# Moving the second half of a weight conversion from the MLP of batch 0 into the attention

## The chip, the core and the metric

The program runs on one NeuronCore of a Trainium2 chip. The metric is the device time of one execution in microseconds (us). The core has five engines with a queue of instructions each: TensorE (PE; its weight loads are listed apart, as PEld), VectorE (DVE), ScalarE (ACT), GpSimd (POOL) and SyncE (SP, which here only starts DMA transfers). An engine takes its instructions in the order of its queue and waits on semaphores for what the others produce. TensorE writes to PSUM, which has eight banks; DVE and ACT read it from there.

## What is computed

The reference is a hash-bucketed attention followed by an FNet block, for 4 batches, 8 heads, 768 positions and 64 dimensions a head:

```
q_bits = (q @ proj) > 0;  k_bits = (k @ proj) > 0        # 6 bits each
mask   = bucket(q) == bucket(k)
attn   = softmax(where(mask, q k^T / 8, -1e9));  o = attn @ v
x  = o as (batch, 768, 512)
u  = x + real(fft over positions and channels of x)
un = (u - mean) / sqrt(var + 1e-6)
out = u + relu(un @ w_ch1) @ w_ch2                       # 512 -> 2048 -> 512
```

The two weight matrices reach the kernel as float64. The kernel reads them as pairs of 32-bit integers and makes float32 of them itself.

## The kernel before

**Two phases.** `attention` handles 16 pairs of heads (n = 0 to 15, four for each batch). Then come, for each of the four batches, `mix` (the Fourier transforms as matmuls, L1045) and `mlp7` (L1342). The MLP multiplies 2x2 blocks with seven products instead of eight (Strassen-Winograd). `inner` makes the hidden layer (L1400), `outer7` the output (L1279); each runs twice per batch, for the first and the second half of the hidden features: inner half 0, outer half 0, inner half 1, outer half 1.

**Order.** The attention is emitted under a manual schedule: every engine executes its instructions in the order in which the code emits them. A pair has six steps, c = 0 to 5. In a step TensorE computes the bucket masks and the scores of 128 keys against all queries (L846, L856), ACT turns them into exponentials in a ring of four buffers `pk` (L862), TensorE multiplies the exponentials of the step before by v (L872), and DVE adds those to a running sum (`tally`, L929). Between these lie, at set steps, the end of the pair before (`scale`: ACT copies at c = 0, TensorE sums at c = 1, reciprocals at c = 2, for batches 0 and 1 the division at c = 3) and the preparation of the next pair (`prepare`: DVE transposes q at c = 0 and k at c = 1, ACT squares q at c = 1 and k at c = 2, TensorE asks for the bits of q at c = 2 and of k at c = 3, DVE tells them one step later). PSUM is full: two score tiles of two banks, two output banks, and two banks (`ps_1`) for everything else. Outside the attention the framework's planner arranges the instructions of each engine by its own costs; `in_turn` ties a weight step behind the last MLP instructions recorded in `done_by`.

**Weights.** `w1` (512 x 2048) comes in 16 slices of 128 x 512, four for each group of 512 columns. `Arrival` keeps transfers of 512 KB ahead in a few raw buffers. `convert` turns one raw slice into float32 with `narrow` (L610): two DVE operations on the high words (L622, L626), three ACT operations (L630, L632, L633, the last with an accumulator read), and, one visit later, a DVE integer addition (L636). After four slices `centred` subtracts the column averages: four matmuls `ws` (L651), an ACT copy to `part`, one matmul `wm` (L659), and four DVE subtractions (L665) in two visits. A generator gives out one such step at a visit: two visits for a slice, four for the centring of a group.

The generator `other` in the attention is `weights1`, on the groups at columns 0 and 1024. It is visited once at the head of pair 1 (where its first transfers start) and at c = 0 and c = 5 of every later pair. The groups at 512 and 1536 are in `weights2`, between the two halves of w2: in batch 0, outer half 0 visits it twice at each of its eight yields. Its transfers go out on the POOL queue. The left factors of inner half 1 (`quarters(HF // 2)`, L1479) need them.

**Fold.** `fold(b)` (L956) makes even and odd parts of a batch's x for the Fourier transform, on DVE, in eight steps for batch 0. The attention visits `fold(0)` at c = 1 from pair 5 on; the folds of later batches run in the MLP of the batch before. `fold` and `part` share one buffer, tag `ef`.

Of the kernel before, what the change touches and what calls it, by code (L numbers as in the profile page):

```python
# [11 lines left out]
F32 = mybir.dt.float32  # L12
# [8 lines left out]
P = 128  # L21
B, H, S, D = 4, 8, 768, 64
NBITS = 6
DM = H * D
DFF = 4 * DM
NT = S // P
NPAIR = H // 2
# [3 lines left out]
NDC = DM // P  # L31
GTT = 2
GT = GTT * P
WC = 512
# [443 lines left out]
def _main(  # L478
# [13 lines left out]
    nc = tc.nc  # L492
# [11 lines left out]
    def wt(shape, dtype, tag, name, bufs=2):  # L504
        return work.tile(shape, dtype, tag=tag, name=name, bufs=bufs)
# [140 lines left out]
    def average(f):  # L646


        ps = pt([P, WC], f"ws{f}")
        for c in range(NDC):  # L650
            nc.tensor.matmul(  # L651
                ps[32 * c : 32 * c + 32, :], ones, w1[:, c, f : f + WC],
                start=True, stop=True,
            )
        part = wt([P, 2, S], F32, "ef", f"part{f}", 1)[:, 0, 0:WC]
        nc.scalar.copy(part, ps)
        yield
        ps = pt([P, WC], f"wm{f}")
        nc.tensor.matmul(ps, mean, part, start=True, stop=True)  # L659
        yield ps  # L660
# [9 lines left out]
    @contextmanager  # L670
    def in_turn():

        with ExitStack() as st:
            for ins in done_by.values():
                st.enter_context(tc.issue_after(ins.ins))
            yield
# [35 lines left out]
    def slices1(fs):  # L712
        return [
            (w1[:, c, f : f + WC], moe_w_ch1[c * P : (c + 1) * P, f : f + WC])
            for f in fs
            for c in range(NDC)
        ]

    def centred(f):

        avg = average(f)
        next(avg)
        yield
        ps = next(avg)
        yield
        for c in range(0, NDC, 2):
            centre(f, ps, (c, c + 1))
            yield

    def weights1():  # L730
        fs = (0, DFF // 2)
        slices = slices1(fs)
        zt = at_([P, 3, 2 * WC], F32, "zraw", "zraw1", 1)
        arrival = Arrival(slices, [zt[:, i] for i in range(3)], 0, nc.sync)
        for i in range(arrival.depth):
            arrival.fetch(i)
        yield
        for i in range(len(slices)):
            low = wt([P, WC], I32, "u", f"low{i}")
            yield from arrival.convert(i, low)  # L740
            yield
            if i % NDC == NDC - 1:
                yield from centred(fs[i // NDC])
# [248 lines left out]
    def attention(other):  # L992

        pending, ends = [], []
        load(1, "qk")
        for n in range(NPAIR * B):
            b, t = divmod(n, NPAIR)
            if t == 0:
                xs[b] = wt([P, NPAIR, S], F32, "x", f"x{b}", B)
            if n + 2 < NPAIR * B:  # L1000
                load(n + 2, "qk")
            if n + 1 < NPAIR * B:
                load(n + 1, "v")
            if n == 1:
                next(other)
            if n == NPAIR + 1:
                folds = fold(0)
            if n == 6:
                nc.sync.dma_start(ch, cn["ch"].ap())
                nc.sync.dma_start(sq, cn["sq"].ap())  # L1010
            ahead = prepare(n + 1) if n + 1 < NPAIR * B else iter(())
            oos = [ps_o.tile([P, 512], F32, tag="o", name=f"oo{n}_{g}") for g in range(2)]
            acc = at_([P, 2, 2, HALF], F32, "acc", f"acc{n}")
            first = None
            for c in range(NT):
                pk = scores(n, c)
                first = pk if c == 0 else first
                done = pending.pop(0) if pending else None
                if c == 1:
                    next(ends[0][0], None) if ends else None  # L1020
                if done:
                    m, d, dpk, doos, dfirst, dacc = done
                    values(m, d, dpk, doos)
                    tally(d, dpk, dfirst, dacc)
                    if d == NT - 1:
                        ends.append([scale(m, doos, dacc, None)])
                        next(ends[-1][0])
                if ends and c in (2, 3):
                    next(ends[0][0], None)
                    if c == 3:  # L1030
                        ends.pop(0)
                if c < NT - 1 if n else c:
                    next(ahead, None)
                if n > 1 and c in (0, NT - 1):
                    next(other, None)
                if n > NPAIR and c == 1:
                    next(folds, None)
                pending.append((n, c, pk, oos, first, acc))
        m, d, dpk, doos, dfirst, dacc = pending.pop(0)
        values(m, d, dpk, doos)  # L1040
        assert next(other, 0) == 0 and next(folds, 0) == 0
        for _ in scale(m, doos, dacc, dpk):
            pass
# [103 lines left out]
    HF = NFC // 2  # L1147
# [53 lines left out]
    def weights2():  # L1201

        slices = []
        for half in range(2):
            for r in range(HF // 2):
                for hi, first in ((0, B11), (1, B21)):
                    c = half * HF // 2 + r + hi * HF

                    step = 1 if hi else T1 - B11
                    dst = w2f[:, 0 : 7 * QB].rearrange("p (i r n) -> p i r n", i=7, n=HD)  # L1210
                    slices.append(
                        (dst[:, first : first + step + 1 : step, r],
                         moe_w_ch2[c * P : (c + 1) * P, :])
                    )
        fs = (WC, DFF // 2 + WC)
        n1 = len(fs) * NDC
        slices[HF:HF] = slices1(fs)
        arrival = Arrival(slices, [zt2[:, i] for i in range(2)], n1, nc.gpsimd)
        for half in range(2):
            if half == 0:  # L1220
                for i in range(arrival.depth):
                    arrival.fetch(i)
                yield
            else:
                for i in range(n1):
                    with in_turn():
                        for _ in arrival.convert(HF + i):
                            pass
                    yield
                    if i % NDC == NDC - 1:  # L1230
                        steps = centred(fs[i // NDC])
                        while True:
                            with in_turn():
                                if next(steps, 0) == 0:
                                    break
                            yield
            for i in range(HF):
                with in_turn():
                    for _ in arrival.convert(half * (HF + n1) + i):
                        pass  # L1240
                yield
                if i % 2:
                    b11, b21, b22, t4, t1, t2, t3 = (q[:, i // 2] for q in right7)
                    with in_turn():
                        nc.vector.tensor_tensor(t3, b22, t1, op=ALU.subtract)
                        nc.vector.tensor_tensor(t1, t1, b11, op=ALU.subtract)
                        nc.vector.tensor_tensor(t2, b22, t1, op=ALU.subtract)
                        nc.vector.tensor_tensor(t4, b21, t2, op=ALU.subtract)
            for i in range(7):
                nc.sync.dma_start(bd[half, i], right7[i])  # L1250
            if half == 0:
                yield
# [89 lines left out]
    def mlp7(b):  # L1342
# [134 lines left out]
        for half in range(2):  # L1477
            if b == 0 and half:
                quarters(HF // 2)  # L1479
            for i, _ in enumerate(inner(half)):  # L1480
                if b == 0 and half and i % 3 < 2:
                    next(arrival2, None)
                yield
            if b == 0 and half == 0:
                for T in range(3):
                    across(b, T, ut[T])
            if b == 0 and half == 0:
                ahead, per = islice(arrival2, 2 * (NDC + 4)), 2
            elif half == (b == 0) and b < B - 1:
                ahead, per = fold(b + 1), 1  # L1490
            else:
                ahead, per = iter(()), 0
            for _ in outer7(b, half, hall, ut, rs, ss):
                for _ in range(per):
                    next(ahead, None)
                yield
            for _ in ahead:
                pass
# [13 lines left out]
    for b in range(B):  # L1512
# [22 lines left out]
        if b == 0:  # L1535
            zt2 = wt([P, 3, 2 * WC], F32, "z", "zraw2", 1)
            arrival2 = weights2()
# [48 lines left out]
```

## Time and profile before

| | us |
|---|---|
| median of 3 runs (1059.22 to 1062.81) | 1059.47 |
| the profiled execution | 1059.36 |
| its span, first to last instruction | 1057.6 |
| TensorE busy | 1031.1 (97%) |
| VectorE busy | 677.3 (64%) |
| ScalarE busy | 500.4 (47%) |
| GpSimd busy | 69.4 (7%) |

In the rows that follow, a line of the timeline or of the chain gives start and duration in us, engine, source line, operation, output<-input and count, and in brackets the idle time before it with what ended it. A row of a table by stretches gives the stretch (us from the start of the span), its length, the busy time of PE, PEld, DVE, ACT and POOL with the number of instructions, the clock granted to TensorE (1.00 is full), the busy share of the DMA engines and the rate. A row of groups gives line, engine, operation, tiles, shapes and count, then busy us and mean ns of one, then idle us before them.

### The profile page before, as it was taken

How to read it: one execution, taken by the hardware profiler on the slowest of the kernel's cores; microseconds unless marked ns; L12 is line 12 of the kernel's file. 1: busy time of each engine (PE TensorE's matmuls, PEld its weight loads, DVE VectorE, ACT ScalarE, POOL GpSimd, SP SyncE). 2: the span in 40 equal slices, each digit the busy share in tenths (PEclk: the TensorE clock that was granted, in tenths of full speed). 3: DMA queues.
4: the chain of work that ended last, by engine and by line, in shares of the span. 5: the costliest groups of instructions: out<-in, count | busy, mean ns of one | idle time of the engine just before them, and what ended most of it. 6: DMA issues, size and time to landing. Idle time of an engine off the chain costs nothing.

```text
span 1057.6 us, 14425 instructions
## 1 busy us (share of the span) xinstructions
PE 1031.1 (97%) x5169; PEld 646.0 (61%) x5169; DVE 677.3 (64%) x1214; ACT 500.4 (47%) x1009; POOL 69.4 (7%) x147
## 2 busy tenths in 40 slices
PE   8999999999999999889999999999999999999997
PEld 4333333333333655555688587689678589678576
DVE  4777878887665398848988854446854354644353
ACT  5677766877666567526513512402521512430420
POOL 2000000000000001200020200020200012200000
PEclk9999999999999999989999999999999999999999
DMA  9534442434210137344642305323314315223301
GB/s 136 119 78 94 83 103 45 101 59 82 46 39 13 41 125 257 99 128 133 245 134 101 98 18 187 92 71 132 92 45 160 105 41 174 70 70 112 107 20 43
DMA packets 172464, 103.03 MB, mean 97 GB/s; under 512 B 126304, under 2 KB 159584, under 8 KB 172384
## 3 DMA queue, kind: packets, MB, share of 16 engines
q1 hardware_dynamic: 165216, 83.92, 29.5%
q0 software_dynamic: 5600, 17.70, 5.6%
q8 instruction: 43, 0.70, 0.3%
q10 hardware_dynamic: 1568, 0.39, 0.2%
q14 instruction: 37, 0.30, 0.1%
HBM read 81.01 MB, written 20.97 MB: 96 GB/s over the span
## 4 chain that ended last, share of the span: by engine, by line
PE 53%; DVE 3%; DMA 2%; ACT 1%; issue 1%; DVEq 0%
PE o L1279 26%; PE h_p L1400 21%; PE cs L1061 2%; PE B L1090 1%; PE A L1090 1%; DMA zraw<-in_moe_w_ch_dram 1%; PE un L1116 1%; PE ws L651 1%; DVE w L626 0%; DMA ad<-tq 0%; PE wm L659 0%; DVE w L1291 0%; DVE w L639 0%; DVE u L1291 0%; DVE w L622 0%
## 5 line engine op out<-in xcount | busy, mean ns | idle before, releaser
L1279 PE MATMUL o<-w,h 128*128 128x256 f32 x1152 | 256.1, 381 | 0.5 <-ACT tq L1298 0.3
L1279 PEld LDWEIGHTS o<-w,h 128*128 128x128 f32 x1152 | 220.2, 191 | 33.8 <-issue 1.5
L862 ACT ACTIVATE pk<-sc 128x768 f32<-128x768 f32 x192 | 153.6, 810 | 91.7 <-PE sc L856 91.7
L1400 PE MATMUL h_p<-x,w 128*128 128x384 f32 x448 | 160.5, 488 | 2.0 <-ACT h L1440 1.8
L856 PE MATMUL sc<-qt,kt 64*128 64x384 f32 x768 | 155.2, 483 | 0.0
L872 PE MATMUL oo<-pk,vn 128*64 128x385 f32 (+1 forms) x768 | 145.1, 498 | 0.0
L929 DVE TENSOR_TENSOR acc<-acc,pk 128x1536 f32<-128x1536 f32 x63 | 110.2, 1750 | 38.6 <-ACT pk L862 38.5
L1400 PEld LDWEIGHTS h_p<-x,w 128*128 128x128 f32 x448 | 84.0, 190 | 60.4 <-ACT h L1440 6.7
L1400 PE MATMUL h_p<-w 128*128 128x384 f32 x288 | 104.8, 487 | 0.0
L872 PEld LDWEIGHTS oo<-pk,vn 128*64 128x64 f32 x768 | 46.7, 136 | 87.8 <-issue 76.8
L856 PEld LDWEIGHTS sc<-qt,kt 64*128 64x128 f32 x768 | 68.6, 189 | 21.7 <-issue 21.5
L1400 PEld LDWEIGHTS h_p<-w 128*128 128x128 f32 x288 | 54.5, 190 | 37.4 <-PE un L1116 0.4
L1291 DVE SCALAR_TENSOR_TENSOR w<-o,rs,w 128x256 f32<-128x256 f32 x56 | 26.9, 481 | 65.6 <-PE o L1279 64.8
L846 PE MATMUL sc<-qkb 64*128 64x384 bf16 x384 | 63.9, 328 | 1.0 <-ACT pk L862 0.5
L846 PEld LDWEIGHTS <-qkb 64*128 64x128 bf16 x384 | 18.8, 93 | 73.0 <-issue 58.6
L1309 ACT COPY tq<-o 128x256 f32<-128x256 f32 x24 | 8.9, 371 | 103.3 <-PE o L1279 103.3
L1414 ACT ACTIVATE h<-h 128x384 f32<-128x384 f32 x72 | 37.7, 524 | 33.6 <-DVE h L1456 14.1
L929 DVE TENSOR_TENSOR acc<-pk,pk 128x1536 f32<-128x1536 f32 x16 | 28.1, 1759 | 39.8 <-ACT pk L862 39.8
L1298 ACT COPY tq<-o 128x256 f32<-128x256 f32 x24 | 8.8, 367 | 74.3 <-PE o L1279 74.3
L1451 DVE TENSOR_TENSOR h<-h 128x384 f32<-128x384 f32 x32 | 17.8, 557 | 40.4 <-ACT h L1450 40.4
L1279 PE MATMUL o<-w 128*128 128x256 f32 x176 | 41.6, 380 | 0.0
L1440 ACT COPY h<-h_p 128x384 f32<-128x384 f32 x32 | 15.2, 476 | 46.1 <-PE un L1116 24.0
(158 smaller groups left out, 1308.8 us busy)
## 6 DMA issues: line engine op xcount, KB each, us to landing
w<-ad SPq DMA_DIRECT2D x168, 128.0 KB, 2.0
w<-bd SPq DMA_DIRECT2D x42, 512.0 KB, 4.6
zraw<-in_moe_w_ch_dram POOLq DMA_DIRECT2D x24, 512.0 KB, 4.3
bd<-w SPq DMA_DIRECT2D x14, 512.0 KB, 3.5
vn<-in_v_dram SPq DMA_DIRECT2D x32, 192.0 KB, 3.0
qn<-in_q_dram SPq DMA_DIRECT2D x116, 48.0 KB, 2.3
kn<-in_k_dram SPq DMA_DIRECT2D x58, 96.0 KB, 3.0
zraw<-in_moe_w_ch_dram SPq DMA_DIRECT2D x8, 512.0 KB, 4.0
```

What stands on the lines that cost most here:

```text
L846: nc.tensor.matmul(ps[:, h, 0:HALF], qk[rows, 1, at : at + P], qk[rows, 0, g * HALF : (g + 1) * HALF], start=start, stop=not start,)
L856: nc.tensor.matmul(ps[:, h, 0:HALF], kt[rows, ks], qt[rows, qs], start=early, stop=not early,)
L862: nc.scalar.activation(pk[:, g, :, 0:HALF], ps[:, :, 0:HALF], AF.Exp, scale=SCALE)
L872: nc.tensor.matmul(oos[g][h * D : (h + 1) * D, 0:w], nat["v", n][:, (2 * c + h) * D : (2 * c + h + 1) * D], pk[:, g, h, 0:w], start=(c == ...
L929: nc.vector.tensor_tensor(acc, (first[:, :, :, 0:HALF] if c == 1 else acc), new, op=ALU.add)
L1061: nc.tensor.matmul(ps[:, pc + 2 * lo : pc + 2 * hi - 1 : 2], z[:, cp, pc, par, t * P : (t + 1) * P], ch[:, cp, pc, lo:hi], start=(cp == 0) ...
L1090: nc.tensor.matmul(ps[:, cols], F[:, par, k, t, j * P : (j + 1) * P], sq[:, t, k, cols], start=(t == 0), stop=(t == 1),)
L1279: nc.tensor.matmul(ps, a[:, r], right7[i][:, r], start=start and r == 0, stop=r == HF // 2 - 1, skip_group_check=not start,)
L1291: nc.vector.scalar_tensor_tensor(t[:, cols], src, r, t[:, cols], op0=ALU.mult, op1=ALU.add)
L1400: nc.tensor.matmul(ps, left[:, k], right[i][:, k], start=start and k == 0, stop=k == 1, skip_group_check=not start,)
L1414: done_by[ET.Activation] = nc.scalar.activation(h, h, AF.Relu)
L1451: done_by[ET.DVE] = nc.vector.tensor_tensor(c22, c21, c22, op=ALU.add)
```

## The change

`weights1` takes all 16 slices, and the attention visits it at c = 0, 1, 4 and 5 of a pair, from c = 4 of pair 1 on. `weights2` keeps only w2, and outer half 0 of batch 0 visits nothing. `part` moves from the buffer `ef` to tag `u`, which has two buffers and which it shares with `low`. `fold(0)` starts in pair 9 instead of 5, with one visit at c = 1 of each pair and a second one in pairs 13, 14 and 15 (at c = 5, 4 and 3).

```diff
@@ average
-        part = wt([P, 2, S], F32, "ef", f"part{f}", 1)[:, 0, 0:WC]
+        part = wt([P, WC], F32, "u", f"part{f}", 2)
@@ weights1
-        fs = (0, DFF // 2)
+        fs = range(0, DFF, WC)
@@ attention
-            if n == NPAIR + 1:
+            if n == 2 * NPAIR + 1:
                 folds = fold(0)
...
-                if n > 1 and c in (0, NT - 1):
+                if n and c in (0, 1, 4, 5) and n + c > 2:
                     next(other, None)
-                if n > NPAIR and c == 1:
+                if n > 2 * NPAIR and (c == 1 or n + c == 18):
                     next(folds, None)
@@ weights2
-        fs = (WC, DFF // 2 + WC)
-        n1 = len(fs) * NDC
-        slices[HF:HF] = slices1(fs)
-        arrival = Arrival(slices, [zt2[:, i] for i in range(2)], n1, nc.gpsimd)
+        arrival = Arrival(slices, [zt2[:, i] for i in range(2)], NDC * DFF // WC, nc.gpsimd)
         for half in range(2):
             if half == 0:
...
-            else:
-                for i in range(n1):
-                    with in_turn():
-                        for _ in arrival.convert(HF + i):
-                            pass
-                    yield
-                    if i % NDC == NDC - 1:
-                        steps = centred(fs[i // NDC])
-                        while True:
-                            with in_turn():
-                                if next(steps, 0) == 0:
-                                    break
-                            yield
             for i in range(HF):
                 with in_turn():
-                    for _ in arrival.convert(half * (HF + n1) + i):
+                    for _ in arrival.convert(half * HF + i):
                         pass
@@ mlp7
-            if b == 0 and half == 0:
-                ahead, per = islice(arrival2, 2 * (NDC + 4)), 2
-            elif half == (b == 0) and b < B - 1:
-                ahead, per = fold(b + 1), 1
-            else:
-                ahead, per = iter(()), 0
+            ahead = fold(b + 1) if half == (b == 0) and b < B - 1 else iter(())
             for _ in outer7(b, half, hall, ut, rs, ss):
-                for _ in range(per):
-                    next(ahead, None)
+                next(ahead, None)
                 yield
```

## The prediction, made before the changed kernel was built or run

> **What bounds the kernel now.** I read the page's head first, for the engine that fills the span.
>
> ```profile
> span 1057.6 us, 14425 instructions
> PE 1031.1 (97%) x5169; PEld 646.0 (61%) x5169; DVE 677.3 (64%) x1214; ACT 500.4 (47%) x1009; POOL 69.4 (7%) x147
> ```
>
> TensorE is busy 97% of the time, so a change pays only where TensorE waits or runs slowly, or where it saves matmuls. The next view is the table by stretches, cut where the stages of batch 0 begin and end: outer half 0 (417.31 to 476.44), two pieces of it, inner half 1 after it, and as the yardstick outer half 0 of batch 1, which has the same products and no weight work.
>
> ```profile
> 417.31:476.44 59.13, 50.60 (x191) 34.78 (x190) 39.98 (x83) 23.02 (x47) 10.93 (x20) 0.88 0.43 139
> 428.76:438.55 9.79, 5.49 (x12) 1.00 (x12) 6.91 (x15) 4.80 (x9) 4.45 (x9) 0.83 0.39 116
> 450.72:461.23 10.51, 6.74 (x11) 1.34 (x11) 3.83 (x7) 4.81 (x9) 1.06 (x2) 0.65 0.75 236
> 476.44:517.47 41.03, 38.08 (x114) 20.74 (x113) 35.39 (x87) 31.39 (x69) 3.17 (x6) 1.00 0.57 183
> 610.36:646.62 36.26, 36.26 (x170) 31.98 (x169) 17.73 (x35) 4.65 (x12) 0.00 (x0) 1.00 0.24 79
> ```
>
> The stage lasts 59.13 us in batch 0 and 36.26 us in batch 1, where TensorE never pauses. The difference of 22.87 us sits mostly in the two short pieces, which are the two centrings: TensorE is idle for 4.30 and 3.77 us in them and the granted clock falls to 0.83 and 0.65. The waits of TensorE in this stage say for what:
>
> ```profile
> PE ws L651 <- DVE w L636: 6.7, 2, 3.6
> PE wm L659 <- ACT part L656: 1.3, 2, 0.7
> PE o L1279 <- ACT tq L1298: 0.3, 1, 0.3
> ```
>
> The column sums `ws` stand in TensorE's queue and wait for the last slices of their group to be converted (6.7 us), `wm` waits for the copy (1.3 us), and the MLP's products stand behind both. Last, the attention, in stretches from one `sum` matmul to the next, that is one pair each: pairs with one slice (first and fourth row), with a `ws` (second), with a `wm` (third), and one late pair without weights (last).
>
> ```profile
> 99.86:121.19 21.33, 21.33 (x146) 8.29 (x145) 17.74 (x22) 16.18 (x30) 0.00 (x0) 1.00 0.40 82
> 121.19:143.52 22.33, 22.33 (x154) 8.46 (x153) 18.11 (x27) 16.37 (x30) 0.00 (x0) 1.00 0.43 88
> 143.52:165.91 22.39, 22.39 (x149) 8.60 (x147) 18.35 (x23) 14.41 (x26) 0.00 (x0) 1.00 0.43 101
> 187.24:208.57 21.33, 21.33 (x146) 8.30 (x144) 18.06 (x24) 16.15 (x30) 0.00 (x0) 1.00 0.48 106
> 317.33:338.66 21.33, 21.33 (x150) 8.29 (x149) 12.00 (x15) 14.41 (x26) 0.00 (x0) 1.00 0.07 15
> ```
>
> A pair takes 21.33 us with a slice or without: conversions are hidden there, and only the matmuls of the centring lengthen it, `ws` by 22.33 - 21.33 = 1.00 us and `wm` by 22.39 - 21.33 = 1.06 us. DVE has 3 us to spare in a pair with a slice, ACT 5 us.
>
> **The change part by part.** *Outer half 0 of batch 0* loses eight slices and two centrings. What is left is the work of batch 1's stage, so I take 36.26 us: a gain of 22.87 us. At worst the early waits for ACT, and DVE or POOL operations between the products, keep a few tenths per product; with the 0.3 us above in front of four of its products, 1.2 us of the gain stay away. It can't be better than 36.26, since TensorE is busy throughout at full clock.
>
> *Two centrings more in the attention.* TensorE gets 2 x (1.00 + 1.06) = 4.12 us more, at full clock and behind nothing, so they count in full.
>
> *Eight slices more in the attention*, and at other steps. Their price on DVE and ACT:
>
> ```profile
> L622 DVE TENSOR_SCALAR w<-zraw 128x512 int32<-128x512 int32 x32 | 13.2, 412 | 6.2 <-DMA zraw<-in_moe_w_ch_dram 6.0 <-issue 0.2
> L626 DVE SCALAR_TENSOR_TENSOR w<-zraw,w 128x512 int32<-128x512 int32 x32 | 22.0, 688 | 0.5
> L636 DVE CUSTOM_DVE_ANT_0 w<-w,low 128x1024 uint16<-128x1024 uint16 x8 | 5.5, 684 | 0.0
> L665 DVE TENSOR_TENSOR w<-w,wm 128x512 f32<-128x512 f32 x16 | 10.2, 676 | 5.9 <-PE wm L659 5.9
> L911 ACT COPY rr<-rr 32x12 f32<-32x12 f32 x32 | 6.3, 198 | 3.2 <-DVE rr L907 2.9
> L817 ACT COPY qkb<-qkb 32x384 bf16<-32x384 bf16 x32 | 16.3, 509 | 2.4 <-DVE qkb L805 1.8
> ```
>
> A slice is 0.41 + 0.69 + 0.68 = 1.78 us of DVE. A pair now holds up to two, so its DVE load rises from 17.74 or 18.06 to about 19.8 us of 21.33, 93%: full but not over. (From pair 9 on the fold comes on top, but there the divisions of batches 0 and 1 are gone, and the late pair shows 12.00 us without fold and weights.) What TensorE needs of DVE has slack of a step or more, with one exception below.
>
> ACT is closer to the path, since TensorE's next scores need the score tile that the exponential has read. Counting visits in the diff, the three ACT operations of a slice fall on c = 5 and on c = 1 in turn (the first on c = 4 of pair 1). How late may an exponential be? These are neighbouring steps 0 and 1 of pair 8, ACT first:
>
> ```profile
> 184.99 0.16 ACT L882 COPY vs<-oo 128x1 f32<-128x1 f32 x1
> 185.19 1.05 ACT L885 ACTIVATE x<-oo,vs 128x384 f32<-128x384 f32 x2
> 186.13 0.68 ACT L630 ACTIVATE low<-zraw 128x512 int32<-128x512 uint32 x1
> 186.83 0.69 ACT L632 ACTIVATE zraw<-zraw 128x512 f32<-128x512 int32 x1
> 187.56 0.78 ACT L633 ACTIVATE zraw<-zraw,least 128x512 f32<-128x512 f32 x1
> 188.24 0.19 ACT L633 ACTIVATION_READ_ACCUMULATOR zraw<-zraw,least 128x1 f32 x1
> 188.33 1.49 ACT L862 ACTIVATE pk<-sc 128x768 f32<-128x768 f32 x2
> 189.71 0.84 ACT L751 ACTIVATE sq<-qn 128x768 bf16<-128x768 f32 x1
> 190.44 0.20 ACT L751 ACTIVATION_READ_ACCUMULATOR sq<-qn 128x1 f32 x1
> ```
>
> ```profile
> 168.14 0.34 PE L846 MATMUL sc<-qkb 64*128 64x384 bf16 x2
> 169.17 1.62 ACT L862 ACTIVATE pk<-sc 128x768 f32<-128x768 f32 x2 [1.51 <-PE sc L856]
> 174.38 0.61 DVE L805 TENSOR_SCALAR qkb<-bitsq,off 128x384 bf16<-128x384 f32 x1
> 175.25 0.85 PE L798 MATMUL bitsk<-kt,pjw 128*32 128x384 f32 x8
> 185.53 0.34 PE L846 MATMUL sc<-qkb 64*128 64x384 bf16 x2
> 189.47 0.34 PE L846 MATMUL sc<-qkb 64*128 64x384 bf16 x2
> ```
>
> An unhindered exponential starts 169.17 - 168.14 = 1.03 us after its step. In the step that begins at 185.53 it should have started at 186.56; behind the conversion (186.13 to 188.33, 2.20 us) it started at 188.33, 1.77 us late. The next step still began 3.94 us after this one, without a pause. So a lateness of 1.77 us costs nothing in a step of 3.94 us (c = 1, 2, 3), and by the same room 0.78 us less, about 1.0, in one without an extra matmul group (c = 0, 4, 5; 3.16 us as (21.33 - 3 x 3.94) / 3).
>
> Now the worst new run of steps. Room for ACT in a step is its length less the 1.62 us of exponentials: 1.54 or 2.32 us. At c = 5 a conversion, 2.20: late 0.66. At c = 0 the copies of `scale`, 0.16 + 1.05 = 1.21: late 0.33. At c = 1 the square with its read, 0.84 + 0.20, and a conversion, together 3.24: late 1.25. At c = 2 four small copies (4 x 0.198) and a square, 1.83: late 0.76. At c = 3 nothing: on time. At c = 4 two copies of 0.51: on time. The peaks, 0.66 before a short step and 1.25 before a long one, lie under 1.0 and 1.77. From these rows the cost is zero; the room is thin, so I take 1.0 us in all, and as bounds 0 and, if each of the eight conversions at c = 1 cost TensorE what the square beside it takes (1.04 us), 8.3 us. A gain is excluded, since the pairs have no pause to lose.
>
> *The one tight place on DVE.* While `wm`'s bank is kept for the four subtractions, the other bank of the pool serves the rest, and the bits of k wait until those of q are read: 174.99 against a start at 175.25, 0.26 us of slack, in pair 7. The new order keeps the bank from c = 0 to c = 4 in pairs 4, 7, 10 and 13. Pairs 4 and 7 have the division in front as here; the others lack it. Zero, at most an addition's 0.68 us in each of four pairs, 2.7 us.
>
> *Transfers.*
>
> ```profile
> zraw<-in_moe_w_ch_dram SPq DMA_DIRECT2D x8, 512.0 KB, 4.0
> ```
>
> Eight transfers move from POOL's queue to SP's, where they wait for their raw buffer ahead of the q and k loads of the pair after next. Three raw slices are under way and two are used in 21.33 us, against a landing of 4.0 us; the q and k loads are due more than a pair later. Zero.
>
> *`part` and `fold(0)`.* `part` costs the same copy in another buffer. The fold's operations are the same; they end in pair 14, before `mix`. Zero, hidden by DVE's free time above.
>
> *Inner half 1* keeps its w2 slices. Its 41.03 us hold 41.03 - 38.08 = 2.95 us of pauses. The planner may arrange them anew behind a shorter stage: I take no change, bounds 2.95 us either way.
>
> **The sum** against the profiled execution's 1059.36 us (0.11 below the median): 1059.36 - 22.87 + 4.12 + 1.0 = 1041.6 us.
>
> [...]
>
> **The rivals.** *The attention gets crowded.* Lateness of ACT and DVE add up where a conversion, a square and a fold share c = 1. For it: 93% of DVE, 1.25 of 1.77 us used. Against: 18.06 us pairs cost nothing. It adds 8.3 instead of 1.0, perhaps 2.7 besides: 1048.9 to 1051.6 us. Still faster.
>
> *The freed stage doesn't shrink fully,* because the planner now puts other work (quarters, the fold of batch 1) between its products or pushes it into inner half 1. Against: batch 1 runs its fold there at 36.26. With the 1.2 and 2.95 us above: 1045.8 us.
>
> *ACT on the path, slower than before.* ACT's queue is strict, so an exponential waits behind a whole conversion. If the 1.77 us were at the very end of the room, and the visits at c = 5 and c = 1 had none left, each of 16 conversions would stop TensorE for its full 2.20 us: 35.2 us, and 1059.36 - 22.87 + 4.12 + 35.2 = 1075.8 us. The decisive point is (22.87 - 4.12) / 16 = 1.17 us a conversion. Against: the visits at c = 0 in the present kernel cost nothing.
>
> [...]
>
> *It doesn't do what it says:* the conversions are still unfinished when the MLP starts and `quarters` waits for them. The visits speak against it: 49 are needed (1 + 16 x 2 + 4 x 4) and 58 offered (1 + 2 + 3 + 13 x 4). Then the 22.87 us would only move, and the centrings cost 4.12 as now: about 1059.4 us.
>
> **How the numbers follow.** Forecast (1039 to 1045) 0.68; crowded attention 0.15; stage not fully freed 0.07; no change 0.05; slower 0.05. Time 1041.6 us. The lower end is 1059.36 - 22.87 + 4.12 - 2.95 = 1037.7, and the upper one reaches to the crowded attention, 1050.0; its far end and the last two cases are left out. A change of 0.5% is 5.3 us, about what a measurement of this kernel can tell from none: faster means under 1054.2. Faster 0.90, same 0.05, slower 0.05.
>
> **What would show it.** Right: outer half 0 of batch 0 at 36 to 37.5 us with clock 1.00 and no `ws` or `wm` in the MLP; the time between the first and the last `sum` of a pair's start longer by 4.1 to 5.5 us; pairs still at 21.33, or 22.4 with one centring matmul group; inner half 1 at 38 to 44 us. Wrong: pairs above 21.8 us without centring, with TensorE waiting for ACT's exponentials or DVE's bits; a pause of TensorE at the head of pair 2, where the first raw slices are fresh; or a stage of over 40 us with waits for something that now hides behind the conversions.

## The result and the profile after

The changed kernel takes 1042.43 us (median of four runs, 1041.75 to 1043.48) against 1060.65 us (median of four, 1059.22 to 1062.81) for the kernel before. The ratio is 0.9827, with a 95% interval from 0.9806 to 0.9849: 1.7% less. The profiled execution took 1041.75 us; the forecast was 1041.6 us.

In the changed kernel some lines have moved: the inner products are L1384, the outer ones L1263; the attention's lines are the same. First the head of its page, to be held against the one quoted in the prediction.

```profile
span 1039.9 us, 14388 instructions
PE 1021.0 (98%) x5169; PEld 643.8 (62%) x5169; DVE 680.0 (65%) x1214; ACT 500.3 (48%) x1009; POOL 66.4 (6%) x139
```

The matmuls are the same 5169, and TensorE is busy 10.1 us less with them (1031.1 before): by that much they ran longer, nearly all of it in outer half 0, where the granted clock was 0.88. The other 7.6 of the 17.7 us of span are pauses. Now the table by stretches of the changed kernel: inner half 0, outer half 0, inner half 1 of batch 0, then two pairs of the attention, one with two slices and one with both a `ws` and a `wm`.

```profile
378.70:422.29 43.59, 40.23 (x138) 23.34 (x136) 36.83 (x86) 32.13 (x70) 3.76 (x7) 1.00 0.52 174
422.29:458.57 36.28, 36.28 (x169) 31.95 (x169) 21.19 (x47) 4.89 (x13) 6.50 (x12) 1.00 0.16 67
458.57:499.74 41.17, 37.91 (x113) 20.54 (x113) 35.54 (x87) 31.45 (x69) 3.27 (x6) 1.00 0.56 182
...
123.93:145.26 21.33, 21.33 (x150) 8.30 (x149) 18.78 (x25) 18.13 (x34) 0.00 (x0) 1.00 0.50 105
145.26:168.60 23.34, 23.34 (x156) 8.73 (x154) 17.51 (x22) 16.84 (x31) 0.00 (x0) 1.00 0.67 163
```

Outer half 0 is now 36.28 us of unbroken TensorE at full clock. A pair with two slices takes the same 21.33 us as one without; the pair with both groups of centring matmuls, `ws` and `wm`, takes 23.34 - 21.33 = 2.01 us more, all of it TensorE's own work (23.34 busy).

The attention as a whole is measured from the first `sum` matmul of pair 1 to that of pair 15. The timeline gives for the kernel before

```profile
35.86 0.85 PE L892 MATMUL sum<-acc,ones 128*32 128x384 f32 x8
...
338.63 0.85 PE L892 MATMUL sum<-acc,ones 128*32 128x384 f32 x8
```

and for the changed one

```profile
35.99 0.85 PE L892 MATMUL sum<-acc,ones 128*32 128x384 f32 x8
...
343.38 0.85 PE L892 MATMUL sum<-acc,ones 128*32 128x384 f32 x8
```

that is 302.77 us and 307.39 us. With the stage boundaries of the two tables the whole difference of 17.7 us can be placed:

| stretch | before | after | difference |
|---|---|---|---|
| start to the first `sum` of pair 1 | 35.86 | 35.99 | +0.13 |
| to the first `sum` of pair 15 | 302.77 | 307.39 | +4.62 |
| to outer half 0 of batch 0 | 78.68 | 78.91 | +0.23 |
| outer half 0 | 59.13 | 36.28 | -22.85 |
| inner half 1 | 41.03 | 41.17 | +0.14 |
| to the end | 540.13 | 540.16 | +0.03 |

The attention's +4.62 us are the matmuls of the centrings and one pause of 0.45 us. The list of TensorE's waits in the attention of the changed kernel has a single row:

```profile
PE sc L846 <- ACT pk L862: 0.5, 1, 0.5
```

It is in pair 1. The timeline shows ACT there, and the next scores of TensorE, which wait for the exponential that stands behind a conversion:

```profile
48.78 1.03 ACT L817 COPY qkb<-qkb 32x384 bf16<-32x384 bf16 x2
49.84 0.69 ACT L630 ACTIVATE low<-zraw 128x512 int32<-128x512 uint32 x1
50.55 0.69 ACT L632 ACTIVATE zraw<-zraw 128x512 f32<-128x512 int32 x1
51.34 0.78 ACT L633 ACTIVATE zraw<-zraw,least 128x512 f32<-128x512 f32 x1
52.02 0.19 ACT L633 ACTIVATION_READ_ACCUMULATOR zraw<-zraw,least 128x1 f32 x1
52.11 1.49 ACT L862 ACTIVATE pk<-sc 128x768 f32<-128x768 f32 x2
...
52.96 0.34 PE L846 MATMUL sc<-qkb 64*128 64x384 bf16 x2 [0.45 <-ACT pk L862]
```

This is the very first conversion, the only one that falls on c = 4, behind the two copies of `qkb`.

### The profile page after: what moved, and what is told of

It reads as the page before. It is cut to its first block, busy times and chain, and to the rows that moved or that the text cites. A ratio compares the mean times of both kernels' runs of the same rounds, so it can differ in the third digit from the quotient of the medians.

```text
span 1039.9 us, 14388 instructions
## 1 busy us (share of the span) xinstructions
PE 1021.0 (98%) x5169; PEld 643.8 (62%) x5169; DVE 680.0 (65%) x1214; ACT 500.3 (48%) x1009; POOL 66.4 (6%) x139
## 4 chain that ended last, share of the span: by engine, by line
PE 91%; DVE 4%; ACT 2%; DMA 2%; issue 1%; DVEq 0%; ACTq 0%
PE o L1263 28%; PE h_p L1384 23%; PE oo L872 13%; PE sc L856 12%; PE sc L846 4%; PE cs L1061 3%; PE B L1090 2%; PE A L1090 2%; PE sum L892 1%; PE bitsq L798 1%; PE bitsk L798 1%; PE un L1116 1%; DMA zraw<-in_moe_w_ch_dram 1%; DVE w L626 1%; DVE w L639 0%
## 5 line engine op out<-in xcount | busy, mean ns | idle before, releaser
L1263 PE MATMUL o<-w,h 128*128 128x256 f32 x1152 | 253.9, 379 | 0.0
L1263 PEld LDWEIGHTS o<-w,h 128*128 128x128 f32 x1152 | 219.0, 190 | 31.0
L1384 PE MATMUL h_p<-x,w 128*128 128x384 f32 x448 | 160.4, 488 | 2.0 <-ACT h L1424 1.8
L1384 PEld LDWEIGHTS h_p<-x,w 128*128 128x128 f32 x448 | 83.9, 190 | 60.4 <-ACT h L1424 6.7
L1384 PE MATMUL h_p<-w 128*128 128x384 f32 x288 | 104.7, 486 | 0.0
L1384 PEld LDWEIGHTS h_p<-w 128*128 128x128 f32 x288 | 54.4, 190 | 37.5 <-PE un L1116 0.4
L1275 DVE SCALAR_TENSOR_TENSOR w<-o,rs,w 128x256 f32<-128x256 f32 x56 | 26.9, 481 | 72.4 <-PE o L1263 71.7
L1263 PE MATMUL o<-w 128*128 128x256 f32 x176 | 41.6, 379 | 0.0
```

The costliest lines, as they stand in the source:

```text
L1263: nc.tensor.matmul(ps, a[:, r], right7[i][:, r], start=start and r == 0, stop=r == HF // 2 - 1, skip_group_check=not start,)
L1275: nc.vector.scalar_tensor_tensor(t[:, cols], src, r, t[:, cols], op0=ALU.mult, op1=ALU.add)
L1384: nc.tensor.matmul(ps, left[:, k], right[i][:, k], start=start and k == 0, stop=k == 1, skip_group_check=not start,)
```

## The experiments

Apart from the two kernels at the end, each experiment is a single execution, and the four of the kernel before differ by 3.6 us among themselves. So the readings go by stages: from the first `sum` of pair 1 to that of pair 15, called the attention below, the changed kernel and two experiments that leave its time as it is took 307.39, 307.39 and 307.38 us. Outer half 0 with its centrings has one trace only, the 59.13 us of the prediction.

The theory: the stage lost 22.87 us to the centrings (their matmuls, what they wait for, and the clock that falls with it, to 0.83 and 0.65 in their two pieces) and to conversions between the products; in the attention the same conversions cost nothing because ACT may be late by a certain room in each step. The rivals: the attention is crowded and has no room left, or the MLP doesn't shrink by itself.

**What the centrings cost in the MLP.** In the kernel *before*, the centring of the groups at columns 512 and 1536 is left out; the conversions stay where they were.

```diff
 weights2
-                        steps = centred(fs[i // NDC])
-                        while True:
-                            with in_turn():
-                                if next(steps, 0) == 0:
-                                    break
-                            yield
+                        for _ in range(4):
+                            yield
```

> The kernel before, without the centring of the two groups that are converted in outer half 0 of batch 0 (columns 512 to 1023 and 1536 to 2047 of w1 stay uncentred; the eight conversions and their visits stay). Theory: what lengthens outer half 0 is the column sums that stand in TensorE's queue and wait, and the clock they cost. Then the stage goes from 59.1 us to between 36.3 and 40.1 us (the first 48 products took 1.1 us too long, so at most 168 / 48 x 1.1 = 3.8 us stay), at clock 1.00, up to 4 us may come back at the head of inner half 1 where the last slices are needed, and the whole takes 1037 to 1044 us. Rival: it is the conversions' load on ACT and DVE between the products; then only the centring's own 4.1 us of matmuls go, the stage stays near 55 us, the whole near 1055 us.

Measured: 1043.89 us, beside 1059.87 for the kernel before on that chip. The row of outer half 0, and below it the one of a piece of it:

```profile
417.04:460.27 43.23, 38.75 (x170) 32.70 (x169) 32.77 (x72) 21.08 (x45) 10.85 (x20) 0.96 0.59 190
436.08:439.46 3.38, 3.38 (x9) 2.70 (x10) 2.26 (x7) 0.57 (x1) 0.52 (x1) 0.57 0.81 276
```

The stage falls from 59.13 to 43.23 us: 15.9 of the 22.87 us go when the centrings alone are left out, more than the 4.12 us of their matmuls by pauses and lowered clock (0.88 with the centrings, 0.96 without). (The conversions alone were not left out; taken away first, they might show another price.) But 43.23 is above what the theory gave. The other 43.23 - 36.28 = 6.95 us are 43.23 - 38.75 = 4.48 us of pauses and 2.47 us of slower matmuls. The waits of TensorE in this kernel (its outer products are L1275) and the timeline say for what: first the waits,

```profile
PE o L1275 <- ACT tq L1294: 3.7, 2, 2.3
...
PE o L1275 <- ACT tq L1305: 0.7, 1, 0.7
```

then the longest of them, ACT first:

```profile
432.16 0.69 ACT L630 ACTIVATE zraw<-zraw 128x512 int32<-128x512 uint32 x1 [2.16 <-DMA zraw<-in_moe_w_ch_dram]
...
435.67 0.36 ACT L1294 COPY tq<-o 128x256 f32<-128x256 f32 x1
...
436.08 3.38 PE L1275 MATMUL o<-w,h 128*128 128x256 f32 x8 [2.34 <-ACT tq L1294]
```

ACT waits 2.16 us for a raw slice to land, works on conversions from 432.16, and only then, at 435.67, reaches the copy of a product that TensorE needs. So the conversions had a price of their own in the MLP. Is it the landing of the raw slices?

**A third raw buffer in the MLP.** The same kernel with three raw buffers for `weights2` instead of two (the third place held a temporary of the outer products, which moves into a larger `bt`); the centring is left out as above.

```diff
-arrival = Arrival(slices, [zt2[:, i] for i in range(2)], n1, nc.gpsimd)
+arrival = Arrival(slices, [zt2[:, i] for i in range(3)], n1, nc.gpsimd)
-    bt = late.tile([P, 2, S], F32, tag="bt", name="bt")
+    bt = late.tile([P, 3, S], F32, tag="bt", name="bt")
-for at in (bt[:, 0], bt[:, 1], zt2[:, 2, 0:S])
+for at in (bt[:, 0], bt[:, 1], bt[:, 2])
```

> The kernel before without the centring of the two late groups (these columns stay uncentred), and with three raw buffers instead of two for the slices of the MLP phase. Theory: what stays of outer half 0 without the centring (43.2 us against 36.3) is ACT waiting for a raw slice (10.9 us) with the copies of the products queued behind it; with one more transfer under way the stage goes to 37 to 40 us. Rival: the 2.3 us of ACT work of a conversion in front of a copy is enough by itself; the stage stays at 42 to 44 us.

Measured: 1042.62 us (1060.85 before on that chip), with outer half 0 at 41.33 us:

```profile
418.75:460.08 41.33, 37.54 (x171) 31.51 (x170) 32.70 (x72) 21.03 (x45) 10.85 (x20) 1.00 0.62 199
```

ACT's wait for transfers in this stage was, with two buffers,

```profile
ACT zraw L630 <- DMA zraw<-in_moe_w_ch_dram: 10.9, 4, 3.3
```

and is now

```profile
ACT zraw L630 <- DMA zraw<-in_moe_w_ch_dram: 6.1, 4, 2.5
```

The 41.33 us lie between the two expectations: 1.9 of the 6.95 us go with the earlier transfers, 5.05 stay. Of the 1.9 us only 0.69 are pauses (4.48 with two buffers, 41.33 - 37.54 = 3.79 with three); 1.21 are matmuls that run faster, with a longest pause of 1.4 us instead of 2.34 and the clock at 1.00 instead of 0.96. Some of the 5.05 us are still waits for transfers (6.1 us on ACT), some ACT's own work in front of the copies; how they divide stays open.

**What the centrings cost in the attention.** In the *changed* kernel, the same two centrings left out.

```diff
 weights1
-                yield from centred(fs[i // NDC])
+                if fs[i // NDC] % (2 * WC):
+                    for _ in range(4):
+                        yield
+                else:
+                    yield from centred(fs[i // NDC])
```

> The changed kernel, without the centring of the groups at columns 512 and 1536 (these stay uncentred; conversions and visits stay). Theory: in the attention the centring costs its matmuls alone, 2 x 2.06 = 4.12 us. From the first sum of pair 1 to that of pair 15 it goes from 307.3 to 303.2 us, the whole from 1041.75 to about 1037.6 us. Rival: the ACT copy and the four subtractions crowd those pairs; then more than 5 us go.

Measured: 1037.23 us, and the attention 303.29 us instead of 307.39: 4.10 us less. The row of a stretch of that length, which begins 0.5 us later:

```profile
35.90:339.20 303.30, 302.84 (x2044) 117.25 (x2036) 249.03 (x330) 233.07 (x417) 0.00 (x0) 1.00 0.42 92
```

TensorE's idle time, 303.30 - 302.84 = 0.46 us, is the pause of pair 1 and was there with the centrings too: they add their matmuls and nothing else. So leaving out the same two centrings saves 15.9 us in the MLP and 4.1 in the attention.

**The place of the fold.** `fold(0)` put back to pair 5, one visit a pair, beside all sixteen slices.

```diff
-            if n == 2 * NPAIR + 1:
+            if n == NPAIR + 1:
-                if n > 2 * NPAIR and (c == 1 or n + c == 18):
+                if n > NPAIR and c == 1:
```

> The changed kernel with the fold of batch 0 back in pairs 5 to 15, one visit a pair as before. Theory: the fold is hidden by DVE's free time and its place is worth nothing: 307.3 us from the first sum of pair 1 to that of pair 15, within 0.3 us. Rival (DVE crowded in pairs 5 to 8, where divisions, two slices and the fold's 2 us meet: 19.8 + 2 = 21.8 us of DVE in a pair of 21.33): 0.5 us and more in each of up to four pairs, 309 us.

Measured: 1042.67 us, the attention 307.39 us to the hundredth. The fold's move is worth nothing in time; the 1 us more of the whole lies ahead of the attention, whose first `sum` comes at 36.95 us instead of 35.99.

**The visits one step earlier.** One visit more, at c = 0 of pair 2, moves all later work by one visit: the conversions stand at c = 4 and c = 0 in turn instead of c = 5 and c = 1.

```diff
-                if n and c in (0, 1, 4, 5) and n + c > 2:
+                if n and c in (0, 1, 4, 5) and (n > 1 or c > 1):
```

> The changed kernel with the visit at c = 0 of pair 2 no longer skipped, so that the conversions fall on c = 0 and c = 4 instead of c = 5 and c = 1; same work, same count of visits. Theory (ACT's room in a step decides): at c = 4 the two copies of 0.51 us and the conversion of 2.20 us exceed the room of 1.54 us by 1.68 us, against about 1.0 us that a short step forgives, so TensorE waits 0.5 to 0.7 us at each of seven more such steps: 3.6 to 4.8 us more, 310.9 to 312.1 us from the first sum of pair 1 to that of pair 15 instead of 307.3, the whole 1045.4 to 1046.6 us. Rival (only the total load of ACT or DVE counts): 307.3 us, 1041.8 us.

Measured: 1045.16 us, the attention 310.53 us (+3.14). The waits of TensorE in it, and one of the eight pauses:

```profile
PE sc L846 <- ACT pk L862: 3.1, 8, 0.4
```

```profile
74.13 0.34 PE L846 MATMUL sc<-qkb 64*128 64x384 bf16 x2 [0.40 <-ACT pk L862]
```

Every conversion at c = 4 costs a pause of 0.36 to 0.45 us, a little less than expected, and about 0.07 us more in which TensorE's matmuls take longer (21.40 us busy in such a pair instead of 21.33), though ACT and DVE do exactly the same work as in the changed kernel. The pause in pair 1 is thus the price of the place and not of the beginning. By the prediction's reckoning the exponential after c = 4 is late by 1.02 for the copies + 2.20 for the conversion - 1.54 = 1.68 us; less the pause, a short step forgives 1.23 to 1.32 us.

**More work for ACT.** One ACT operation of each conversion (L632, 0.69 us) is done twice, and in another kernel three times; the diff shows the first. Each of the sixteen conversions gets longer by 0.69 and by 1.38 us.

```diff
             nc.scalar.activation(t, hi, AF.Abs)
+            nc.scalar.activation(t, hi, AF.Abs)
```

> The changed kernel with the absolute value of each conversion taken twice on ACT, 0.69 us more on each of 16 conversions, 11.0 us in all. Theory (ACT's room in a step decides): at c = 5 the lateness becomes 2.89 - 1.54 = 1.35 us against about 1.0, at c = 1 it becomes 0.67 + 1.04 + 2.89 - 2.32 = 2.28 us against 1.77 or somewhat more; TensorE waits 0.35 us eight times, 0 to 0.5 us eight times and 0.7 us once: 3.5 to 7.5 us, 310.8 to 314.8 us from the first sum of pair 1 to that of pair 15. Rival (ACT is busy 76% there and hides it): 307.3 us. If ACT had no room at all: 11.0 us more, 318.3 us.

Measured: 1043.20 us; the attention 309.73 us (+2.34), less than expected.

> The changed kernel with the absolute value of each conversion taken three times on ACT, 1.38 us more on each, 22.1 us in all. The room of a short step, corrected by the two earlier doses (lateness 1.68 paused TensorE 0.38, 2.37 paused it 1.15 us), is 1.2 to 1.3 us. Theory: lateness after c = 5 is 3.58 - 1.54 = 2.04 us, a pause of 0.74 us at each of seven steps, 1.8 us in pair 1, and after c = 1 it is 1.30 + 1.21 - 1.54 + 1.04 + 3.58 - 2.32 = 3.27 us against a room of at least 2.0 (1.25 + 0.78): 0 to 1.2 us at each of eight steps. Together 7.0 to 16.6 us of pauses, all for exponentials, 313.9 to 323.5 us from the first sum of pair 1 to that of pair 15. Rival (only ACT's total counts, 85% busy with it): under 310 us.

Measured: 1055.03 us (1060.85 before on that chip); the attention 319.77 us (+12.4). The waits of TensorE in the attention, with +0.69 us,

```profile
PE sc L847 <- ACT pk L863: 2.0, 3, 1.1
```

and with +1.38 us:

```profile
PE sc L847 <- ACT pk L863: 11.8, 15, 1.8
```

Of the first 11 us of added time 2.3 come through, of the second 11 us 10: a threshold, as the theory wants it. Its place can be read three times from pair 1. The lateness there is 1.68, 2.37 and 3.06 us, the pause 0.45, 1.15 and 1.84 us: the room of a short step is 1.23, 1.22 and 1.22 us. With +0.69 us the lateness behind c = 5 is 0.66 + 0.69 = 1.35 us, 0.13 above that room, and five pairs in which the list shows no pause take 21.46 to 21.48 us instead of 21.33. With +1.38 us TensorE pauses there for 0.77 to 0.81 us (0.66 + 1.38 - 1.23 = 0.81), and for 0.38 to 0.41 us behind c = 1. In three pairs of this kernel the pause behind c = 5 is 1.28 to 1.39 us, and in two of the one with +0.69 us it is 0.41 and 0.42: there ACT's copies of `qkb` at c = 4, which the prediction's reckoning has on time, wait 0.93 to 1.19 us for DVE, so that the exponential ahead of the conversion is late already. Behind c = 1 the exponential is late by 1.23 - 0.33 = 0.90 us from c = 0, and by 0.90 + 3.24 + 1.38 - 2.32 = 3.20 us after c = 1, so a long step forgives about 2.8 us.

**More work for DVE.** The operation of L626 twice, and in another kernel four times: 0.69 and 2.06 us more per slice on DVE; the diff shows the first.

```diff
             di, hi, -(1 << 30), di, op0=ALU.bitwise_and, op1=ALU.bitwise_or
         )
+        if apart:
+            nc.vector.scalar_tensor_tensor(
+                di, hi, -(1 << 30), di, op0=ALU.bitwise_and, op1=ALU.bitwise_or
+            )
```

> The changed kernel with one DVE operation of each conversion (the merge of the sign bits, 0.69 us) done twice, 11.0 us of DVE in all; a pair with two slices then holds about 21.2 us of DVE in 21.33. Theory (a step or more of slack on DVE, ACT's room decides): 0 to 3 us more, 307.3 to 310.3 us from the first sum of pair 1 to that of pair 15. Rival (DVE is as close to the path as ACT): 8 to 11 us more, 315 to 318 us.

Measured: 1042.94 us, the attention 307.38 us: 11 us more of DVE cost nothing.

> The changed kernel with the merge of the sign bits of each conversion done four times on DVE, 2.06 us more on each, 33 us in all. Theory (TensorE needs DVE only a step or more later, so DVE costs nothing until its total over the three pairs of a group nears the time of those pairs): DVE goes from 254 to about 287 us of 307, 93%; 0 to 5 us more from the first sum of pair 1 to that of pair 15, 307.4 to 312.5 us. Rival (DVE is on the path now that a pair with two slices holds 24 us in 21.33): 2.6 us in each of eight such pairs and more, above 325 us.

Measured: 1051.23 us, the attention 316.59 us (+9.2), between the two expectations, which both missed. DVE is too late here, but TensorE hardly waits for DVE itself. (Of the +9.2 us, 6.9 are pauses; the other 2.3 are matmuls that run longer, most of them behind the longest pause, where the clock is 0.65 for 3.79 us and 0.94 for 6.00 us more.) The waits of TensorE in this attention:

```profile
PE sc L850 <- ACT pk L866: 6.3, 7, 2.2
PE sum L896 <- DVE acc L933: 0.9, 2, 0.4
PE bitsk L802 <- DVE rt L903: 0.2, 1, 0.2
```

and the longest in the timeline, ACT first:

```profile
223.67 0.83 ACT L915 COPY rrs<-rrs 32x12 f32<-32x12 f32 x4 [4.84 <-DVE rrs L911]
...
225.36 1.49 ACT L866 ACTIVATE pk<-sc 128x768 f32<-128x768 f32 x2
...
226.21 0.34 PE L850 MATMUL sc<-qkb 64*128 64x384 bf16 x2 [2.21 <-ACT pk L866]
```

ACT's copies of the reciprocals wait 4.84 us for DVE, the exponential stands behind them until 225.36 though its scores (L860) were done at 221.45, and TensorE pauses 2.21 us for the exponential. DVE's lateness reaches TensorE through ACT's queue.

**Two mends.** The profile after leaves two things to take: the pause of 0.45 us in pair 1, and inner half 1, where DVE is busy for 35.54 of 41.17 us and TensorE pauses. In the next kernel the first conversion waits for c = 5 (the visit that it gives up comes back at c = 0 of pair 2), and `quarters(HF // 2)` moves ahead of outer half 0, where DVE is now busy for only 21.19 of 36.28 us; for this the quarters get a buffer of their own instead of `tq`, which the outer products use.

```diff
-                if n and c in (0, 1, 4, 5) and n + c > 2:
+                if n and c in (0, 1, 4, 5) and (n > 1 or c == 5):
+    stq = late.tile([P, 2, 4, HD], F32, tag="stq", name="stq")
-        st = tq[:, 0:4].rearrange("p i (k m) -> p i k m", m=P)
+        st = stq[:, f % 2].rearrange("p i (k m) -> p i k m", m=P)
-                    left = tq[:, i - S2].rearrange("p (k m) -> p k m", m=P)
+                    left = stq[:, f % 2, i - S2].rearrange("p (k m) -> p k m", m=P)
 mlp7
-            if b == 0 and half:
-                quarters(HF // 2)
...
                 for T in range(3):
                     across(b, T, ut[T])
+                quarters(HF // 2)
```

> The changed kernel, first conversion at c = 5 of pair 1 instead of c = 4, and the quarters of batch 0 in two buffers of their own, the first ones of inner half 1 emitted ahead of outer half 0. Theory: the pause of 0.45 us in pair 1 goes; at the head of inner half 1 the wait for the quarters (4.3 us of DVE after the last product) and the DVE wait of 1.0 us for their transfer go: 3.3 us of pauses in that stage become about 1, so 0.5 + 2 to 3 us less, 1038 to 1039.5 us. Rival (DVE's 35.5 us of work in 41.2 us bound the stage anyway, only 1.7 us of them move): 1040 to 1041 us.

Measured: 1036.70 us (median of four, 1036.40 to 1037.44) against 1061.54 before on that chip, a ratio of 0.9773 with an interval from 0.9757 to 0.9789, which lies below that of the changed kernel: this one beats both. Inner half 0, outer half 0 and inner half 1 of batch 0:

```profile
378.00:420.15 42.15, 40.18 (x138) 23.51 (x137) 38.20 (x90) 32.25 (x70) 3.77 (x7) 1.00 0.57 178
420.15:456.41 36.26, 36.26 (x169) 31.92 (x169) 21.19 (x47) 4.90 (x13) 6.50 (x12) 1.00 0.23 88
456.41:494.23 37.82, 37.26 (x114) 20.78 (x113) 32.99 (x79) 31.14 (x69) 3.28 (x6) 1.00 0.52 170
```

Inner half 1 gains 41.17 - 37.82 = 3.35 us, inner half 0 1.44, the attention 307.39 - 306.88 = 0.51, more than expected in all. The later batches gave 0.6 us back, which was not followed further. In inner half 0 no quarters were moved, so the gain there goes with the buffers of their own: TensorE's wait of 1.4 us for quarters (`tq`, L1177) is in the trace of the changed kernel and not in this one. Whether inner half 1 gained by DVE's earlier work or by these buffers was not taken apart; TensorE's waits for quarters, 1.3 us there, are gone too.

**The w2 slices earlier too.** The same kernel, with the conversion of w2 beginning at the first step of `mix`, in raw buffers of its own.

```diff
-            zt2 = wt([P, 3, 2 * WC], F32, "z", "zraw2", 1)
+            zt2 = late.tile([P, 3, 2 * WC], F32, tag="zraw2", name="zraw2")
-            other = after(NT - 2, other, islice(arrival2, HF + 2))
+            other = after(0, other, islice(arrival2, HF + 2))
```

> As the one before, and the raw buffers of w2 in memory of their own, so that its conversion can start with the first step of mix instead of the fifth. Theory: inner half 0 of batch 0 (43.6 us against 39.2 us in batch 1) holds the first eight conversions on DVE (36.8 us busy); started in mix, where DVE is busy 9.2 of 17.6 us, about half of the 4.4 us comes back: 2 us less than the one before, 1036 to 1037.5 us. Rival: the conversions delay the x updates in mix by as much: no gain or a loss of 1 to 2 us against the one before.

Measured: 1041.71 us (median of four, 1041.06 to 1042.87), 5 us slower than without this step. The expectation's rival had the direction, but its size was too small. A pause at the head of inner half 0 is 1.1 us in the kernel without the step (first line) and 2.39 us here:

```profile
384.03 2.82 PE L1385 MATMUL h_p<-bt,stq 128*128 128x384 f32 x8 [1.12 <-DVE bt L1364]
...
387.18 5.46 PE L1385 MATMUL h_p<-bt,stq 128*128 128x384 f32 x8 [2.39 <-DVE bt L1364]
```

with the row of these matmuls in the table by stretches:

```profile
387.18:392.64 5.46, 5.46 (x9) 3.04 (x10) 4.00 (x8) 1.04 (x2) 0.00 (x0) 0.50 0.37 126
```

The pause is only 1.3 us longer, but the clock is 0.50 behind it, and the eight matmuls take 2.64 us more. Between the two profiled executions 2.24 us lie ahead of these matmuls (from the `sum` of pair 15 on, this pause among them) and 0.92 us ahead of the first `sum` of pair 1, where the step changes nothing; the last section comes back to these.

## Why the prediction was right, point by point

- **Outer half 0 at 36.26 us, no less and no more.** Measured 36.28 at clock 1.00. Taking the same stage of another batch as the yardstick held. The prediction said that the 22.87 us sat mostly in the centrings and didn't divide them; the runs, with the centrings left out first, divide them into 15.9 for the centrings and 6.95 for the conversions, 2.47 of these by matmuls that ran longer. My theory of the first experiment, that the conversions alone were nearly free there, fell.
- **Two centrings more, 4.12 us.** Measured 4.10 by leaving them out, and all of it TensorE's own matmuls.
- **Eight slices more, 1.0 us taken between 0 and 8.3.** Measured 0.50: 307.39 - 302.77 - 4.12. The mechanism was right, and two sizes in it were off. The room of a short step, taken as "about 1.0", is 1.22 to 1.32 us, and that of a long one, taken as 1.77 because that much had been seen to be free, is about 2.8. And the chosen worst run, c = 5 to c = 2, was not the worst: the conversion at c = 4 of pair 1, which the text names, was not worked out. The same sum gives 1.68 us late there, above the room, and the only pause of the attention. By the room that the prediction took, about 1.0, that place alone would have given 0.68 us. The 1.0 us was taken because the room looked thin, not for this place; that it covered what came is luck.
- **The tight place on DVE, 0.** The trace lists no wait of TensorE for DVE in the attention. DVE's load in a pair, 18.78 us where two slices fall together, was forecast at about 19.8.
- **Transfers, `part` and `fold(0)`, 0.** No pause of TensorE for a transfer in the attention; the fold's place is worth nothing by experiment.
- **Inner half 1 unchanged.** 41.17 against 41.03. It had 3.35 us to give, but to another change.
- **The rivals.** *Crowded attention*: no, though it comes when a conversion is 1.38 us longer on ACT. *ACT on the path*: the price was 0.5 / 16 = 0.03 us a conversion against the decisive 1.17; with +1.38 us it is (12.4 + 0.5) / 16 = 0.81, still short of it. *Freed stage not shrinking* and *the work only moves*: no, by 36.28 and 41.17.
- **The sum**, 1059.36 - 22.87 + 4.12 + 1.0 = 1041.6 against the profiled 1041.75. The 0.5 us too much for the slices stands against 0.5 us of small differences elsewhere (+0.13, +0.23, +0.14, +0.03), which no step named. So the mechanism was right stage by stage, but the hit to 0.1 us is in part chance.

## What to carry to other kernels

How busy an engine is in a stage does not tell whether work fits in: the same conversions cost 0.5 or 3.6 us in the attention (307.39 or 310.53 - 302.77 - 4.12) by one step of difference. What tells is how late the instruction behind may be, and that is worked out step by step, for every place a piece of work gets, the first one included, and with the small operations counted that wait for another engine. A stage that is freed of work should be looked at again for what can now be put into it, as the quarters show (with buffers of their own), while work brought ahead of a busy start can cost more than the pause it makes, as the w2 slices show (1.3 us more of pause, and 2.64 us more for the eight matmuls behind it at 0.50).

## What the runs showed of the hardware

In the kernel before, the granted clock was 0.52 and 0.50 behind the two pauses of 3.62 and 3.10 us in outer half 0, in the stretches of the `ws` matmuls that follow them:

```profile
433.44:436.90 3.46, 3.46 (x4) 0.36 (x4) 3.46 (x9) 2.45 (x6) 1.20 (x3) 0.52 0.18 26
...
454.87:458.70 3.83, 3.82 (x4) 0.36 (x4) 1.67 (x3) 2.58 (x6) 1.06 (x2) 0.50 0.60 127
```

It fell behind shorter pauses too. A pause of 2.34 us was followed by 3.38 us at 0.57 (centring left out), one of 2.39 us by 5.46 us at 0.50 (w2 earlier), and the one of 2.21 us in the attention with more DVE work by 3.79 us at 0.65:

```profile
226.21:230.00 3.79, 3.79 (x18) 1.66 (x19) 3.32 (x6) 2.87 (x5) 0.00 (x0) 0.65 0.65 104
```

Behind the pause of 1.84 us with more ACT work the clock stayed full:

```profile
54.89:60.00 5.11, 5.11 (x36) 2.38 (x39) 4.39 (x5) 4.39 (x8) 0.00 (x0) 1.00 0.82 171
```

These measurements don't give a limit on the length of the pause: at the start of the program, ahead of pair 1, pauses shorter than this one were followed by a low clock. In the kernel with more ACT work it was 1.48 us:

```profile
7.64 1.21 PE L774 MATMUL trk<-ident,kn 128*128 128x128 f32 x6 [1.48 <-DMA kn<-in_k_dram]
...
7.80:11.80 4.00, 3.99 (x24) 1.53 (x25) 1.85 (x5) 1.34 (x4) 0.00 (x0) 0.57 1.30 166
```

At the same place a pause of 1.70 us (w2 earlier) was followed by 0.60 in the same four microseconds, and one of 1.74 us (quarters earlier) by 1.00. The chain has the eight `bitsq` matmuls there take 1.55 us and end at 10.71 in the one, and take 0.90 us and end at 9.80 in the other; this is where the 0.92 us between these two executions come from. What decides besides the last pause stays open. What the clock is worth shows in the pair of kernels that differ in the w2 slices: behind 2.39 us of pause eight matmuls took 5.46 us at 0.50, behind 1.1 us they took 2.82 us in a stage that has 1.00.
